# Sums of squares kept in PSUM, GpSimd adding pairs of chunks, and a softmax mixed with the first fold

## The chip, the core and the metric

The kernel runs on one core of one Trainium2 chip. The time is the device time of one execution in microseconds (us); the kernel before was run three times. A profiled execution of the same program gives the trace from which all rows below come. The engines are TensorE (PE, with its weight loads as PEld), VectorE (DVE), ScalarE (ACT), GpSimd (POOL) and SyncE (SP), which issues the loads.

## What is computed

A channel attention over 6016 tokens of 256 channels, and then two feed-forward layers:

```python
qn = q / (np.linalg.norm(q, axis=1, keepdims=True) + 1e-06)   # norm over the tokens
kn = k / (np.linalg.norm(k, axis=1, keepdims=True) + 1e-06)
s = kn.transpose(0, 2, 1) @ qn / tau                          # 256 x 256 scores
a = np.exp(s - s.max(-1, keepdims=True))
a /= a.sum(-1, keepdims=True) + 1e-09
x = (v @ a).reshape(B * S, D)
g = x @ w_gate                                                # first layer, 256 -> 1536 -> 256
x = silu(g) * (x @ w_val) @ w_out
h = x @ w_in                                                  # second layer, 256 -> 2048 -> 256
out = (h * np.clip(h + 3.0, 0.0, 6.0) / 6.0) @ w_out
```

The weights come as 64-bit floats and are turned into 32-bit ones on the chip.

## The kernel before

The order of each engine's instructions is written out by hand: the program issues them in the order of the code, and nothing reorders them.

**Prologue.** `q` and `k` come in 47 tiles of 128 tokens, grouped in 18 chunks (of 1, 2, 2, then thirteen of 3, then 2 and 1 tiles), numbered from 0. Eight chunks are under way at a time; SyncE issues them on one queue, with the first weight blocks between them. For each chunk ScalarE writes the squares of `tq` and `tk` into a tile `sq`, VectorE adds `sq` to the accumulator `acc` (128 x 1536 for a full chunk), and TensorE multiplies `tk` by `tq` into the scores `s` (two products a tile, each of which shows as two MATMUL records). VectorE folds `acc` from three tiles to one at the end. TensorE then adds over the partitions (`ss`), while the last tiles' score products wait behind it (three tiles; the constant `AFTER_SS`). From `ss` come the norms (ScalarE's root, VectorE's reciprocals `rno` and diagonal `dg`), TensorE spreads them over the partitions (`bc`, copied by ScalarE to `bc_sb`), VectorE scales the scores and takes the row maxima, ScalarE the exponentials, TensorE transposes them half by half (`tp`, copied to `et` in the tile `early`), and *folds* the attention matrix into the first weights (`ps_a`, `ps_d`), so that `v @ a` is never computed on its own.

**Weight blocks.** A block of 64-bit weights (`raw`, a job) passes through steps: `cut` (two VectorE instructions that take exponent `e` and mantissa `m` apart), `power` (two ScalarE instructions on `e`), `mantissa` and `sign` (VectorE on `m`), together the `fields`, and `scale` (VectorE, `m` times `e`). The function `pump` starts the fields of the next block; `PUMP_AT` says behind which chunk. Two blocks are needed for the first fold, the third and fourth soon after.

**The stretch after it.** The first layer starts with a plain product over 24 units, with later folds and weight blocks between them, and goes on in the seven-product scheme for two by two blocks for both layers. TensorE carries every product as three passes of 32-bit halves.

Of the kernel before, what the change touches and what calls it, by code (L numbers as in the profile page):

```python
# [18 lines left out]
def channel_attention_then_two_ffns(  # L19
# [24 lines left out]
    nc = tc.nc  # L44
# [405 lines left out]
    with tc.manual_schedule():  # L450

        with tc.tile_pool(name="sm", bufs=1) as sm, tc.tile_pool(name="qk", bufs=AHEAD) as qk_p, tc.tile_pool(
            name="sqp", bufs=3
        ) as sq_p:
            QC = 3
# [16 lines left out]

            LOAD_AT = {5: 1, 7: 2}
            PUMP_AT = {5: 1, 7: 2}

            AFTER_SS = 3
            WARM = 3
            ones = sm.tile([P, P], F32, name="ones")
            nc.vector.memset(ones, 1.0)

            def keep_warm(n):

                ps = ps_f.tile([P, P], F32, tag="b0", name="warm")
# [3 lines left out]
            loaded = []  # L487
# [4 lines left out]
            nc.sync.dma_start(out=tau_sb, in_=tau.to_broadcast([P, 1]))  # L492
            ident = sm.tile([P, P], F32, name="ident")
# [6 lines left out]

            s_ps = [ps_acc.tile([P, C], F32, tag=f"acc{i}", name=f"s{i}") for i in range(CT)]
# [36 lines left out]
            def square_sums():  # L538

                ss_ps = ps_acc.tile([P, 2 * CT], F32, tag="acc2", name="ss")  # L540
# [36 lines left out]

            nc.scalar.activation(warm, ones[:, 0:1], AF.Sqrt)
            squares(0)
            for i, (n0, n) in enumerate(chunks):  # L580
                if i + AHEAD < len(chunks):
                    loaded.append(load_qk(i + AHEAD))
                if i + AHEAD == len(chunks):
                    vraw = load_v(0)
                    load_jobs(RAW)
                squares(i + 1)
                sq = sqs.pop(i)
                nc.vector.tensor_tensor(out=acc[:, :n], in0=acc[:, :n], in1=sq[:, :n], op=ALU.add)
                if i == len(chunks) - 2:
                    nc.vector.tensor_tensor(out=acc[:, 1], in0=acc[:, 1], in1=acc[:, 2], op=ALU.add)  # L590
# [19 lines left out]
            bc_ps = ps_acc.tile([P, C], F32, tag="acc3", name="bc")  # L610
# [11 lines left out]
            for c in range(CT):  # L622
# [11 lines left out]
                )  # L634


            def transposed(c):
                tp = ps_f.tile([P, CT, P], F32, tag=f"b{c}", name="tp")
                for d in range(CT):
                    nc.tensor.transpose(tp[:, d, :], ex[:, c, d * P : (d + 1) * P], ident)  # L640
                nc.vector.tensor_scalar(
                    out=et[:, :, c * P : (c + 1) * P], in0=tp, scalar1=1.0, scalar2=None, op0=ALU.mult
                )

# [10 lines left out]

            transposed(0)
            transposed(1)
# [9 lines left out]
            jobs[2].mantissa()  # L667
            jobs[2].sign()
            passed[1] = 3
            load_jobs()  # L670
            nc.scalar.activation(warm, three, AF.Silu)
            jobs[2].power([1])
            passed[2:] = [3, 3]


        w1_p = ctx.enter_context(tc.tile_pool(name="w1", bufs=1))
        h_p = ctx.enter_context(tc.tile_pool(name="h", bufs=5))
        hl_p = ctx.enter_context(tc.tile_pool(name="hl", bufs=4))

# [7 lines left out]
        FA = [op_p.tile([P, 2 * CT, CW], F32, tag=f"op{i}", name="FA") for i in (7, 2)]  # L687
        FS = [op_p.tile([P, 2 * CT, CW], F32, tag=f"op{i}", name="FS") for i in (8, 1)]

        def first_fold():  # L690

            for c, ps in enumerate(fold_ps):
# [12 lines left out]
                v_lo(1, c)  # L705
            jobs[2].scale()
            for c, ps in enumerate(fold_ps):
# [311 lines left out]
        scaling = {i + 1: j for i, j in fields.items()}  # L1019
        third = fields.pop(0)  # L1020
        scaling.pop(1)
# [37 lines left out]
        for i, (f, b) in enumerate(units):  # L1059
# [31 lines left out]
            if i == 1:  # L1091
                jobs[third].power()
                jobs[third].mantissa()
                jobs[third].sign()
                passed[1] += 1
                load_jobs()
# [12 lines left out]
            if i == 0:  # L1109
                jobs[third].cut()  # L1110
            h_of = (f, b, h)
# [121 lines left out]
```

## Time and profile before

| | |
|---|---|
| three runs | 1096.37, 1097.02, 1097.03 us |
| profiled execution | 1096.71 us, span 1094.9 us |
| TensorE busy | 1085.6 us of the span |
| VectorE, ScalarE, GpSimd busy | 800.3, 759.8, 78.0 us |

The span runs from the first to the last instruction; the profiled execution's own time has 1.8 us more around it. Times in the trace count from the span's start. A MATMUL's recorded duration is longer than its share of TensorE, since they overlap; how many stand in a stretch tells more.

### The profile page before, as it was taken

Reading aid. Unit: us, or ns where it says so; the run is one execution under the profiler, and the core shown is the slowest. Engines: PE = TensorE matmul, PEld = TensorE weight load, DVE = VectorE, ACT = ScalarE, POOL = GpSimd, SP = SyncE. Lnnn points to the kernel's source line nnn. Section 1 sums busy time; section 2 is a strip of 40 time slices with the busy share of each in tenths; the row PEclk is TensorE's granted clock in tenths of the full one; section 3 lists DMA queues with packets and bytes.
Section 4 is the critical chain, followed back from the end, with each engine's and each line's share of the span. In section 5 each row is a group of like instructions: output and inputs, shape, how many; then the busy total and the mean of one; then the engine's idle time right before and its main releaser. Section 6 shows DMA issues by size and latency. Waiting matters only on the chain.

```text
span 1094.9 us, 13730 instructions
## 1 busy us (share of the span) xinstructions
PE 1085.6 (99%) x4878; PEld 915.2 (84%) x4878; DVE 800.3 (73%) x1259; ACT 759.8 (69%) x1319; POOL 78.0 (7%) x92
## 2 busy tenths in 40 slices
PE   8999999999999999999999999999999999999998
PEld 7888888888888888888888888888888888888997
DVE  6998995776776777677666677687687687686665
ACT  6776666667667776776765676776776776776765
POOL 0000000112221122122100000000000000000000
PEclk9999999999999999999999999999999999999999
DMA  9533303237346337426664724224225225224100
GB/s 353 214 96 101 111 1 114 76 120 259 106 145 225 109 128 245 146 95 224 211 231 184 305 97 159 91 97 169 82 97 172 79 96 173 73 85 151 39 1 34
DMA packets 63860, 150.31 MB, mean 137 GB/s; under 512 B 5168, under 2 KB 30896, under 8 KB 63024
## 3 DMA queue, kind: packets, MB, share of 16 engines
q1 hardware_dynamic: 63216, 148.67, 38.2%
q8 instruction: 38, 0.62, 0.2%
q10 hardware_dynamic: 576, 0.77, 0.2%
q14 instruction: 30, 0.25, 0.1%
HBM read 89.78 MB, written 59.64 MB: 136 GB/s over the span
## 4 chain that ended last, share of the span: by engine, by line
PE 95%; DMA 4%; DVE 1%; ACT 0%; issue 0%; SPq 0%; DVEq 0%
PE o L112 41%; PE ps_b L112 23%; PE ps_a L112 15%; PE ps_d L112 14%; DMA tk<-in_k 2%; DMA tq<-in_q 1%; PE ps_b L647 1%; DMA raw<-in_moe_w_gate 1%; PE ps_d L647 1%; PE ps_a L647 0%; DVE w L737 0%; DVE early L168 0%; ACT w L732 0%; DVE s_sb L623 0%; DVE nmx L631 0%
## 5 line engine op out<-in xcount | busy, mean ns | idle before, releaser
L875 DVE TENSOR_TENSOR hl<-h,hl 128x512 fp32r<-128x512 f32 (+2 forms) x312 | 210.4, 687 | 156.1 <-ACT hl L809 150.4
L112 PE MATMUL o<-hl,w2o 128*128 128x512 f32 (+1 forms) x1152 | 287.8, 385 | 0.0
L112 PEld LDWEIGHTS o<-hl,w2o 128*128 128x128 f32 x1152 | 215.8, 188 | 41.1 <-DVE hl L875 1.0
L809 ACT ACTIVATE hl<-h 128x512 fp32r<-128x512 f32 (+2 forms) x312 | 187.6, 617 | 58.0 <-DVE h L859 53.5
L112 PE MATMUL o<-hl,wo 128*128 128x496 f32 (+1 forms) x864 | 217.0, 386 | 0.0
L112 PEld LDWEIGHTS o<-hl,wo 128*128 128x128 f32 x864 | 162.2, 188 | 29.7
L112 PE MATMUL ps_b<-op,w 128*128 128x496 f32 (+1 forms) x540 | 139.3, 384 | 0.0
L112 PEld LDWEIGHTS ps_b<-op,w 128*128 128x128 f32 x540 | 101.3, 188 | 18.5 <-ACT ps_b L809 0.4
L112 PE MATMUL ps_b<-op,w2i 128*128 128x512 f32 (+1 forms) x432 | 112.0, 385 | 0.0
L813 DVE TENSOR_TENSOR h<-h,ps_d 128x512 f32<-128x512 f32 (+2 forms) x108 | 72.6, 672 | 51.5 <-PE ps_d L112 48.4
L809 ACT ACTIVATE h<-ps_b 128x512 f32<-128x512 f32 (+2 forms) x108 | 63.5, 588 | 65.6 <-PE ps_b L112 64.6
L809 ACT ACTIVATE ps_b<-ps_a 128x512 f32<-128x512 f32 (+2 forms) x108 | 61.8, 572 | 54.9 <-PE ps_a L112 54.9
L112 PE MATMUL ps_a<-op,w 128*128 128x496 f32 (+1 forms) x360 | 99.2, 384 | 0.0
L112 PE MATMUL ps_d<-op,w 128*128 128x496 f32 (+1 forms) x360 | 99.2, 384 | 0.0
L853 ACT ACTIVATE h<-h,three 128x512 f32<-128x512 f32 (+1 forms) x96 | 68.7, 716 | 40.3 <-DVE h L813 39.0
L112 PEld LDWEIGHTS ps_b<-op,w2i 128*128 128x128 f32 x432 | 81.1, 188 | 15.1
L813 DVE TENSOR_TENSOR h<-h,ps_b 128x512 f32<-128x512 f32 (+2 forms) x108 | 72.6, 672 | 9.9 <-PE ps_b L112 8.1
L112 PE MATMUL ps_a<-op,w2i 128*128 128x512 f32 (+1 forms) x288 | 79.7, 385 | 0.0
L112 PE MATMUL ps_d<-op,w2i 128*128 128x512 f32 (+1 forms) x288 | 79.7, 385 | 0.0
L112 PEld LDWEIGHTS ps_a<-op,w 128*128 128x128 f32 x360 | 67.6, 188 | 12.1
L112 PEld LDWEIGHTS ps_d<-op,w 128*128 128x128 f32 x360 | 67.6, 188 | 12.1
L859 DVE SCALAR_TENSOR_TENSOR h<-h 128x512 f32<-128x512 f32 (+1 forms) x96 | 65.1, 678 | 12.5 <-ACT h L853 12.5
(139 smaller groups left out, 1298.0 us busy)
## 6 DMA issues: line engine op xcount, KB each, us to landing
op<-opd SPq DMA_DIRECT2D x35, 512.0 KB, 4.3
opd<-sp SPq DMA_DIRECT2D x28, 496.0 KB, 2.7
op<-opd SPq DMA_DIRECT2D x28, 496.0 KB, 5.4
opd<-sp SPq DMA_DIRECT2D x21, 512.0 KB, 2.6
raw<-in_moe_w_out SPq DMA_DIRECT2D x14, 512.0 KB, 4.1
w2i<-wi_d SPq DMA_DIRECT2D x4, 1792.0 KB, 7.8
opd<-st SPq DMA_DIRECT2D x14, 512.0 KB, 2.6
x2r<-x_d SPq DMA_DIRECT2D x10, 512.0 KB, 4.7
```

The lines of the kernel that those rows point to most:

```text
L112: nc.tensor.matmul(out, lhsT=w, rhs=x, start=first, stop=last, skip_group_check=True)
L647: nc.tensor.matmul(out, lhsT=et[:, d, c * P : (c + 1) * P], rhs=wf[m, g][:, d, :], start=start and d == 0, stop=d == CT - 1, skip_group_ch ...
L809: nc.scalar.activation(out[:, : self.n], src[:, : self.n], AF.Copy)
L813: nc.vector.tensor_tensor(out=out[:, :n], in0=a[:, :n], in1=b[:, :n], op=ALU.add)
L853: nc.scalar.activation(r[:, : self.n], x[:, : self.n], AF.Relu, bias=three)
L859: nc.vector.scalar_tensor_tensor(out=r[:, :n], in0=r[:, :n], scalar=6.0, in1=x[:, :n], op0=ALU.min, op1=ALU.mult)
L875: nc.vector.tensor_tensor(out=hl[:, 1, :n], in0=h[:, :n], in1=hl[:, 0, :n].bitcast(F32), op=ALU.subtract)
```

## The change

- The accumulator of the squares is a PSUM tile of three banks, `acc_ps`, set to zero by VectorE; the add of chunk 15 writes its sum to the SBUF tile `acc`, and the last two chunks and the folds go on there.
- GpSimd adds the squares of chunk pairs (4,5), (7,8) and (10,11); VectorE adds each sum to `acc_ps` two chunks later.
- Four small matmuls of ones stand first on TensorE, and the three that stood ahead of the transposes are gone.
- The first two weight blocks are loaded behind chunks 8 and 10 instead of ahead of chunks 5 and 7, `tau` behind chunk 9; their fields stand behind chunks 8 and 11, and their `scale`, which stood behind the last add, behind chunks 12 and 13.
- Five tiles' products stand behind `ss` instead of three.
- The third block's `mantissa` and both steps of `power` stand ahead of the scores' scaling, its `sign` and `scale` inside the softmax. The first half is transposed and folded ahead of the second half's exponentials; ScalarE copies its transpose. The fourth block's steps stand earlier.

```diff
-    ps_acc = ctx.enter_context(tc.tile_pool(name="ps_acc", bufs=1, space=PSUM))
...
-            name="sqp", bufs=3
-        ) as sq_p:
+            name="sqp", bufs=6
+        ) as sq_p, tc.tile_pool(name="ps_s", bufs=1, space=PSUM) as ps_s:
...
-            LOAD_AT = {5: 1, 7: 2}
-            PUMP_AT = {5: 1, 7: 2}
-
-            AFTER_SS = 3
-            WARM = 3
+            LOAD_AT = {0: 1, 2: 2}
+            PUMP_AT = {8: 1, 11: 2}
+            SCALE_AT = {12: 0, 13: 1}
+            PAIRED = (5, 8, 11)
+            PAIR_LAG = 2
+
+            AFTER_SS = 5
+            WARM = 4
...
-            for i in range(AHEAD):
-                load_jobs(LOAD_AT.get(i, 0))
-                loaded.append(load_qk(i))
+            keep_warm(WARM)
+            loaded = [load_qk(i) for i in range(AHEAD)]
...
+            acc_ps = ps_s.tile([P, QC, 2, C], F32, tag="acc", name="acc_ps")
+            nc.vector.memset(acc_ps, 0.0)
             acc = sm.tile([P, QC, 2, C], F32, name="acc")
-            nc.gpsimd.memset(acc, 0.0)
...
                 squares(i + 1)
-                sq = sqs.pop(i)
-                nc.vector.tensor_tensor(out=acc[:, :n], in0=acc[:, :n], in1=sq[:, :n], op=ALU.add)
+                if i + 1 not in PAIRED:
+                    sq = sqs.pop(i)
+                    if i in PAIRED:
+                        first = sqs.pop(i - 1)
+                        nc.gpsimd.tensor_tensor(out=first, in0=first, in1=sq, op=ALU.add)
+                        paired[i + PAIR_LAG] = first
+                    else:
+                        a = acc if i > len(chunks) - 3 else acc_ps
+                        out = acc if i >= len(chunks) - 3 else acc_ps
+                        nc.vector.tensor_tensor(out=out[:, :n], in0=a[:, :n], in1=sq[:, :n], op=ALU.add)
+                if i in paired:
+                    nc.vector.tensor_tensor(out=acc_ps, in0=acc_ps, in1=paired.pop(i), op=ALU.add)
...
                 if i in PUMP_AT:
                     pump(PUMP_AT[i], steps=(1,), load=False)
+                    load_jobs(RAW if i > AHEAD else 0)
+                if i in SCALE_AT:
+                    jobs[SCALE_AT[i]].scale()
...
-            jobs[0].scale()
-            jobs[1].scale()
             jobs[2].cut()
+            jobs[2].mantissa()
             v_hi(0)
             v_hi(1)
             norms(ss_ps)
+            jobs[2].power()
...
-            jobs[2].power([0])
             for j, i in tiles[-AFTER_SS:]:
                 matmuls([j], i, [1])
-            keep_warm(WARM)
...
+                if c == 0:
+                    transposed(0)
+                    jobs[2].sign()
+                    passed[1] = 3
+                    load_jobs()
...
+            jobs[2].scale()
             fold_ps = [ps_f.tile([P, 2, CW], F32, tag="ad"[c], name="ps_" + "ad"[c]) for c in range(CT)]
             for c, ps in enumerate(fold_ps):
                 for m in range(2):
 
                     folding(ps[:, m, :], m, 0, c, m == 0)
+                    if not c and not m:
+                        transposed(1)
```

VectorE in the middle of the prologue, before the change: `acc` is the accumulator, `raw` a weight block, its four rows are the fields.

```order
L588 TENSOR_TENSOR acc<-acc,sq 128x1536 x3
L133 TENSOR_SCALAR e<-raw 128x512
L136 TENSOR_SCALAR m<-raw 128x512
L149 SCALAR_TENSOR_TENSOR m<-raw,m 128x512
L155 SCALAR_TENSOR_TENSOR m<-raw,m 128x512
L588 TENSOR_TENSOR acc<-acc,sq 128x1536 x2
```

After the change, from the add of the pair (4,5) (L603 adds a pair, L601 a chunk) to that of the pair (7,8) and the second block's fields:

```order
L603 TENSOR_TENSOR acc_ps<-acc_ps,sq 128x1536
L132 TENSOR_SCALAR e<-raw 128x512
L135 TENSOR_SCALAR m<-raw 128x512
L148 SCALAR_TENSOR_TENSOR m<-raw,m 128x512
L154 SCALAR_TENSOR_TENSOR m<-raw,m 128x512
L601 TENSOR_TENSOR acc_ps<-acc_ps,sq 128x1536
L603 TENSOR_TENSOR acc_ps<-acc_ps,sq 128x1536
L132 TENSOR_SCALAR e<-raw 128x512
L135 TENSOR_SCALAR m<-raw 128x512
L148 SCALAR_TENSOR_TENSOR m<-raw,m 128x512
L154 SCALAR_TENSOR_TENSOR m<-raw,m 128x512
```

The fields stand behind later chunks, and fewer adds stand between them. The end of the adds on VectorE, before the change, from the last eight full chunks to the two `scale` (`early`):

```order
L588 TENSOR_TENSOR acc<-acc,sq 128x1536 x8
L588 TENSOR_TENSOR acc<-acc,sq 128x1024
L590 TENSOR_TENSOR acc<-acc 128x512
L591 TENSOR_TENSOR acc<-acc 128x512
L588 TENSOR_TENSOR acc<-acc,sq 128x512
L597 TENSOR_SCALAR half<-half,tau_sb 128x2
L168 TENSOR_TENSOR early<-m,e 128x512 x2
```

After the change, from the add of chunk 12 to that of chunk 17:

```order
L601 TENSOR_TENSOR acc_ps<-acc_ps,sq 128x1536
L167 TENSOR_TENSOR early<-m,e 128x512
L601 TENSOR_TENSOR acc_ps<-acc_ps,sq 128x1536
L603 TENSOR_TENSOR acc_ps<-acc_ps,sq 128x1536
L167 TENSOR_TENSOR early<-m,e 128x512
L601 TENSOR_TENSOR acc_ps<-acc_ps,sq 128x1536
L601 TENSOR_TENSOR acc<-acc_ps,sq 128x1536
L605 TENSOR_TENSOR acc<-acc 128x512
L601 TENSOR_TENSOR acc<-acc,sq 128x1024
L607 TENSOR_TENSOR acc<-acc 128x512
L601 TENSOR_TENSOR acc<-acc,sq 128x512
```

The two `scale` moved ahead of the last adds, and the pair (10,11) stands between chunks 13 and 14. ScalarE behind `ss`, before the change, from the root to the exponentials of both halves:

```order
L553 ACTIVATE nrm<-ss,tiny 128x4
L554 ACT_TABLE_LOAD
L554 ACTIVATE warm<-tiny 128x1
L613 ACTIVATE bc_sb<-bc 128x256
L143 ACTIVATE e<-e,exp_top 128x512
L632 ACTIVATE s_sb,den<-s_sb,nmx 128x256 x2
```

After the change (L142 and L144 are the third block's `power`):

```order
L554 ACTIVATE nrm<-ss,tiny 128x4
L555 ACT_TABLE_LOAD
L555 ACTIVATE warm<-tiny 128x1
L142 ACTIVATE e<-e,exp_top 128x512
L144 ACTIVATE e<-e,exp_span 128x512
L632 ACTIVATE bc_sb<-bc 128x256
L659 ACTIVATE s_sb,den<-s_sb,nmx 128x256
L642 ACTIVATE early<-tp 128x2x128
L659 ACTIVATE s_sb,den<-s_sb,nmx 128x256
```

Both steps of `power` stand ahead of `bc_sb`, and the copy of the first transpose between the two exponentials.

## Rows read from the trace of the kernel before

**Rows 1.** The page's first part: busy time, share of the span, instructions.

```profile
PE 1085.6 (99%) x4878; PEld 915.2 (84%) x4878; DVE 800.3 (73%) x1259; ACT 759.8 (69%) x1319; POOL 78.0 (7%) x92
```

**Rows 2.** Chain that ended last, first 60 us: start, length, what.

```profile
54.34 2.77 PE ps_b L112 x12
```

**Rows 3.** TensorE's timeline, 42 to 55 us: start, length, what, count.

```profile
44.07 0.95 PE L542 MATMUL ss<-ones,acc 128*128 128x1 f32 x8
46.78 0.71 PE L612 MATMUL bc<-dg,ones 128*128 128x128 f32 x4 [0.36 <-DVE dg L561]
...
50.73 1.89 PE L647 MATMUL ps_a<-early 128*128 128x256 f32 x8
```

**Rows 4.** Score MATMULs alone, by stretch: busy (count), granted clock, DMA.

```profile
3.50:7.90 4.40, 4.32 (x10) 1.00 1.01 362
8.20:22.80 14.60, 14.60 (x69) 1.00 0.99 385
```

**Rows 5.** Timeline, ScalarE's squares of chunks 4, 5, 6, 8 and 12.

```profile
10.47 0.85 ACT L521 ACTIVATE sq<-tq 128x768 f32<-128x768 f32 x1 [0.19 <-DMA tq<-in_q]
...
13.66 0.84 ACT L521 ACTIVATE sq<-tq 128x768 f32<-128x768 f32 x1 [1.48 <-DMA tq<-in_q]
...
15.53 0.84 ACT L521 ACTIVATE sq<-tq 128x768 f32<-128x768 f32 x1 [0.16 <-DMA tq<-in_q]
...
22.18 0.84 ACT L521 ACTIVATE sq<-tq 128x768 f32<-128x768 f32 x1 [1.38 <-DMA tq<-in_q]
...
30.74 0.84 ACT L522 ACTIVATE sq<-tk 128x768 f32<-128x768 f32 x1
```

**Rows 6.** Timeline, VectorE: first block's fields, later adds, last add, two `scale`.

```profile
17.08 0.42 DVE L133 TENSOR_SCALAR e<-raw 128x512 uint32<-128x512 uint32 x1
...
19.21 3.61 DVE L588 TENSOR_TENSOR acc<-acc,sq 128x1536 f32<-128x1536 f32 x2
...
26.87 14.26 DVE L588 TENSOR_TENSOR acc<-acc,sq 128x1536 f32<-128x1536 f32 x8 [0.25 <-ACT sq L522]
...
42.69 0.69 DVE L588 TENSOR_TENSOR acc<-acc,sq 128x512 f32<-128x512 f32 x1
...
43.43 1.28 DVE L168 TENSOR_TENSOR early<-m,e 128x512 f32<-128x512 f32 x2
```

**Rows 7.** GpSimd's groups by shape: count, busy us, mean ns, idle before.

```profile
L209 POOL TENSOR_TENSOR st<-m,st 128x512 fp32r<-128x512 f32 x8 | 10.4, 1295 | 92.8 <-ACT st L215 92.8
...
L209 POOL TENSOR_TENSOR st<-m,st 128x256 fp32r<-128x256 f32 x8 | 6.0, 753 | 80.9 <-ACT st L220 80.9
```

**Rows 8.** Line 866, 270 to 310 us (min/median/max ns); timeline, 299 to 305 us.

```profile
L866 DVE TENSOR_TENSOR h<-h x6: 676/892/1139, 271.3 to 307.8; 128x496 f32<-128x496 f32 x6
...
299.52 0.67 DVE L813 TENSOR_TENSOR h<-h,ps_b 128x496 f32<-128x496 f32 x1
299.61 1.29 POOL L168 TENSOR_TENSOR m<-m,e 128x512 f32<-128x512 f32 x1 [6.04 <-DVE m L155]
...
300.29 1.14 DVE L866 TENSOR_TENSOR h<-h 128x496 f32<-128x496 f32 x1
...
301.83 0.47 POOL L198 TENSOR_TENSOR e<-e,m 128x128 f32<-128x128 f32 x1
...
302.25 0.90 POOL L199 TENSOR_TENSOR e<-m 128x128 f32<-128x128 f32 x1
302.75 0.93 DVE L357 TENSOR_TENSOR sp<-vr,sp 128x496 fp32r<-128x496 f32 x1
```

**Rows 9.** Timeline, ScalarE from the root to `power` of the third block.

```profile
45.05 0.27 ACT L553 ACTIVATE nrm<-ss,tiny 128x4 f32<-128x4 f32 x1 [2.80 <-PE ss L542]
45.34 1.28 ACT L554 ACT_TABLE_LOAD   x1
...
47.53 0.38 ACT L613 ACTIVATE bc_sb<-bc 128x256 f32<-128x256 f32 x1 [0.69 <-PE bc L612]
47.81 0.71 ACT L143 ACTIVATE e<-e,exp_top 128x512 f32<-128x512 uint32 x1
```

More of the change, by code (lines that the diff above doesn't have):

```diff
@@ L481, in keep_warm @@
             def keep_warm(n):
-                ps = ps_f.tile([P, P], F32, tag="b0", name="warm")
+                ps = ps_f.tile([P, P], F32, tag="a", name="warm")
                 for _ in range(n):
                     nc.tensor.matmul(ps, lhsT=ones, rhs=ones, start=True, stop=True)
-            loaded = []
-            for i in range(AHEAD):
-                load_jobs(LOAD_AT.get(i, 0))
-                loaded.append(load_qk(i))
+            keep_warm(WARM)
+            loaded = [load_qk(i) for i in range(AHEAD)]
             tau_sb = sm.tile([P, 1], F32, name="tau_sb")
-            nc.sync.dma_start(out=tau_sb, in_=tau.to_broadcast([P, 1]))
             ident = sm.tile([P, P], F32, name="ident")
@@ L499, in channel_attention_then_two_ffns @@
             nc.gpsimd.memset(exp_span, 4.0 * (EXP_TOP - EXP_LOW))
-            s_ps = [ps_acc.tile([P, C], F32, tag=f"acc{i}", name=f"s{i}") for i in range(CT)]
+            assert QC == 3 and CT * C == TB
+            s_ps = [ps_f.tile([P, C], F32, tag=f"b{i}", name=f"s{i}") for i in range(CT)]
+            acc_ps = ps_s.tile([P, QC, 2, C], F32, tag="acc", name="acc_ps")
+            nc.vector.memset(acc_ps, 0.0)
             acc = sm.tile([P, QC, 2, C], F32, name="acc")
-            nc.gpsimd.memset(acc, 0.0)
             half = sm.tile([P, 2 * CT], F32, name="half")
@@ L538, in square_sums @@
             def square_sums():
-                ss_ps = ps_acc.tile([P, 2 * CT], F32, tag="acc2", name="ss")
+                ss_ps = ps_f.tile([P, 2 * CT], F32, tag="a", name="ss")
                 for m in range(2 * CT):
@@ L578, in channel_attention_then_two_ffns @@
             nc.scalar.activation(warm, ones[:, 0:1], AF.Sqrt)
+            paired = {}
             squares(0)
@@ L582, in channel_attention_then_two_ffns @@
                     loaded.append(load_qk(i + AHEAD))
+                if i == 1:
+                    nc.sync.dma_start(out=tau_sb, in_=tau.to_broadcast([P, 1]))
+                load_jobs(LOAD_AT.get(i, 0))
                 if i + AHEAD == len(chunks):
@@ L586, in channel_attention_then_two_ffns @@
                 squares(i + 1)
-                sq = sqs.pop(i)
-                nc.vector.tensor_tensor(out=acc[:, :n], in0=acc[:, :n], in1=sq[:, :n], op=ALU.add)
+                if i + 1 not in PAIRED:
[10 more added lines that the diff above has]
+                    nc.vector.tensor_tensor(out=acc_ps, in0=acc_ps, in1=paired.pop(i), op=ALU.add)
+                if i == len(chunks) - 3:
+                    nc.vector.tensor_tensor(out=acc[:, 0], in0=acc[:, 0], in1=acc[:, 2], op=ALU.add)
                 if i == len(chunks) - 2:
-                    nc.vector.tensor_tensor(out=acc[:, 1], in0=acc[:, 1], in1=acc[:, 2], op=ALU.add)
                     nc.vector.tensor_tensor(out=acc[:, 0], in0=acc[:, 0], in1=acc[:, 1], op=ALU.add)
@@ L613, in channel_attention_then_two_ffns, with transposed @@
             nc.scalar.activation(bc_sb, bc_ps, AF.Copy)
-            jobs[2].power([0])
             for j, i in tiles[-AFTER_SS:]:
                 matmuls([j], i, [1])
-            keep_warm(WARM)
+            def transposed(c):
+                tp = (ps_s, ps_f)[c].tile([P, CT, P], F32, tag="td"[c], name="tp")
+                for d in range(CT):
+                    nc.tensor.transpose(tp[:, d, :], ex[:, c, d * P : (d + 1) * P], ident)
+                out = et[:, :, c * P : (c + 1) * P]
+                if c == 0:
+                    nc.scalar.activation(out, tp, AF.Copy)
+                else:
+                    nc.vector.tensor_scalar(out=out, in0=tp, scalar1=1.0, scalar2=None, op0=ALU.mult)
             nmx = sm.tile([P, CT], F32, name="nmx")
@@ L634, in channel_attention_then_two_ffns @@
                 )
[L637 to L643, printed above, removed]
+                if c == 0:
+                    transposed(0)
+                    jobs[2].sign()
+                    passed[1] = 3
+                    load_jobs()
             def folding(out, m, g, c, start):
@@ L666, in channel_attention_then_two_ffns @@
             v_lo(0, 1)
[L667 to L670, printed above, removed]
             nc.scalar.activation(warm, three, AF.Silu)
-            jobs[2].power([1])
             passed[2:] = [3, 3]
@@ L677, in channel_attention_then_two_ffns @@
         h_p = ctx.enter_context(tc.tile_pool(name="h", bufs=5))
+        ps_acc = ctx.enter_context(tc.tile_pool(name="ps_acc", bufs=1, space=PSUM))
         hl_p = ctx.enter_context(tc.tile_pool(name="hl", bufs=4))
@@ L688, in channel_attention_then_two_ffns @@
         FS = [op_p.tile([P, 2 * CT, CW], F32, tag=f"op{i}", name="FS") for i in (8, 1)]
+        third = at[1, 1]
         def first_fold():
@@ L705, in first_fold @@
                 v_lo(1, c)
-            jobs[2].scale()
+            jobs[third].cut()
+            jobs[third].mantissa()
             for c, ps in enumerate(fold_ps):
@@ L1019, in channel_attention_then_two_ffns @@
         scaling = {i + 1: j for i, j in fields.items()}
-        third = fields.pop(0)
+        assert fields.pop(0) == third
         scaling.pop(1)
@@ L1091, in channel_attention_then_two_ffns @@
             if i == 1:
-                jobs[third].power()
-                jobs[third].mantissa()
                 jobs[third].sign()
@@ L1109, in channel_attention_then_two_ffns @@
             if i == 0:
-                jobs[third].cut()
+                jobs[third].power()
             h_of = (f, b, h)
```

4 lines of the change are left out of this document (1 added, 3 removed).

## The prediction

> **What bounds the kernel now.** Read the page's first part, then the chain of waits, then each engine's timeline up to the point where TensorE stops waiting. TensorE is busy 99% of the span [rows 1], and the chain in order of time runs on TensorE alone, in pieces that touch, from 54.34 us [rows 2]. So the sum is the shift of that moment: everything that the change touches stands ahead of it or beside a TensorE that is never idle.
>
> Before 54.34 three engines matter. TensorE: the sums `ss` start at 44.07, the broadcast `bc` at 46.78, the first fold at 50.73 [rows 3]. The fold is 6.66 us after `ss` and the steady stretch 10.27 after it. TensorE ran late into `ss`: its first ten score MATMULs fill 4.4 us, 0.43 each, and 69 later ones 14.6, 0.21 each [rows 4]. That is the lower of its two levels against the higher, after a start without work; the granted clock column reads 1.00 in both. VectorE: its last add ends at 43.38 (42.69 + 0.69), and from 26.87 on adds stand back to back, 14.26 us for seven full chunks and one of two tiles, so 1.86 for a full chunk with the gap before it and 1.33 for the other [rows 6]. Loads: a chunk's squares begin when `tq` lands; chunks 5 and 6 are 1.87 us apart, a weight block adds 1.32 (10.47 to 13.66 is 3.19) [rows 5]. From chunk 6 (15.53) to chunk 8 (22.18) are two chunks, one block and 1.59 us more, where `tau` travels [rows 5].
>
> **The change on VectorE ahead of `ss`.** This sets the end, because `ss` needs the finished `acc`.
>
> The bytes ahead of chunk 12 are the same as before, only in another order, so its squares end at 31.6 as now (30.74 + 0.84) [rows 5]. Behind them stand five full adds (chunks 12 and 13, the pair (10,11), 14, 15), 9.3 us; the two `scale`, 1.28; two folds of `acc` at 0.73, 1.46; chunk 16, 1.33; chunk 17, 0.79: together 14.1 us [rows 6]. In the kernel before, four full adds and no `scale` follow chunk 12. Even if VectorE stood ready and idle for chunk 12, `acc` would be done at 45.7, against 43.38. The pairs save three adds, 5.6 us, but they save them where VectorE now waits for loads, and one of them comes back after chunk 12.
>
> I expect VectorE not to be ready. GpSimd's add of 512 elements takes 1.295 us and of 256 0.753 [rows 7], so 1536 take an estimated 1.295 + 4 x 0.542 = 3.46 us. Beside GpSimd, VectorE's instructions with two SBUF inputs wait: `h<-h`, 0.68 at the least, took 1.14 us started at 300.29 under a GpSimd add that ends at 300.90; GpSimd's add at 302.25 waited in turn, 0.90 instead of the 0.47 of its like at 301.83, and the VectorE instruction that came at 302.75 waited behind that one, 0.93 [rows 8]. So the two alternate, whole instruction by whole instruction. The VectorE instruction with a PSUM input at 299.52 kept its 0.67 [rows 8]. The adds into `acc_ps` have one SBUF input and go on beside GpSimd; the weight steps (`cut`, `mantissa`, `sign`, `scale`) work from SBUF to SBUF and don't. No row shows `cut` beside GpSimd. Its bounds: no wait, or the whole rest of the add; I take the wait, as its nearest rows are the SBUF ones.
>
> The Trainium skill (SBUF — State Buffer, "Who interferes with whom") states the same rule against this change: the second port pair of VectorE is GpSimd's, held for a whole instruction, by VectorE instructions with two SBUF inputs and by single-input ones in the two-port modes. The rows agree for two inputs; by the rule `cut` waits too, and the sum is the one below.
>
> With [rows 5] the new order gives chunk 8's `tq` at 10.47 + 4 x 1.87 = 17.95 and its squares done at 19.7 (half a chunk, 0.94, more for `tk`, and 0.84). GpSimd then adds (7,8) from 19.75 to 23.2. The first weight block lands at 20.2, inside that add, so its fields, 2.13 us (17.08 to 19.21) [rows 6], run 23.2 to 25.3 instead of 20.2 to 22.3. Chunk 9 and the pair (7,8), 3.7 us: 29.0. The second block's `cut`, 0.67: 29.7. Chunk 11's squares end at 17.95 + 3 x 1.87 + 2 x 1.32 + 1.59 + 0.94 + 0.84 = 29.6, and GpSimd's add (10,11) wants the port then. Whichever of it and `mantissa` goes first, at least `sign` stands behind 3.46 us of GpSimd and the fields end at 34.1 to 34.5; I take 34.2. Then the 14.1 us: `acc` is done at 48.3, and `ss` starts at 48.4, 4.3 us later than now.
>
> **TensorE ahead of `ss`.** Five tiles instead of three stand behind `ss`, 8 MATMULs of 0.21 less ahead of it, 1.7 us; warm matmuls first save between nothing and 2.1 us (ten MATMULs at 0.43 instead of 0.21) [rows 4]. TensorE is then through by 40.3 to 42.4: hidden, since `acc` is later. But TensorE now stands idle for some 6 us before `ss`, more than the 3.5 us at the start of the span behind which it ran at 0.43 [rows 4]. Price of the lower level, if it lasts 4.4 us again: `ss` 0.8 us more, then six of the ten score MATMULs at 0.43, and `bc` can start 5.3 us behind `ss` instead of 3.1. ScalarE hides part of that (next paragraph): 1.9 us. Its bounds are 0 and 1.9; I take 1.9.
>
> **From `ss` to the steady stretch.** On VectorE `cut` and `mantissa` of the third block (0.7 + 0.7) lie beside `ss` and the square root, where two `scale` (1.28) and `cut` lie now [rows 6]. On ScalarE both steps of `power` now stand ahead of `bc_sb`: root at 0.99 behind `ss`, 0.27; table 1.28; 0.2; two steps of 0.71; `bc_sb` starts 4.15 us behind `ss` instead of 3.46 (47.53 - 44.07) [rows 3, 9], 0.7 later. From `bc_sb` to the first fold are 3.2 us now; by halves it is one row of `s_sb`, maximum, exponential, transpose and copy instead of two maxima in a row: 2.9, 0.3 earlier. The fold itself takes 0.1 more, for the transposes of the second half inside it. Sum: + 0.5.
>
> **At nothing**: the memset of `acc_ps` (VectorE has no other work until the first squares), `tau` and the weight loads in another place (same bytes, same queue), the third block's steps earlier or later beside steady TensorE [rows 2]. Without that cover the third block's `cut` and `mantissa` ahead of the first low parts would cost 1.4 us once.
>
> **Sum**: 4.3 + 0.5 + 1.9 = 6.7 us. The profiled execution took 1096.71 us with a span of 1094.9; its median is 0.3 above, inside the 0.66 by which the runs differ. 1096.7 + 6.7 = 1103.4.
>
> **Rivals.**
> *The lower level doesn't come.* For it: four warm matmuls and a long busy stretch ahead. Against: 6 us without work. 1101.5. The Trainium skill (TensorE: Matmul & The Clock Gate, "What's actually happening") says that an idle TensorE returns to the lower level by default, which would favour my sum.
> *GpSimd doesn't hold the fields*, or the order at 29.6 falls the other way (`cut` runs beside GpSimd, and `sign` is through before the second add). VectorE then waits for chunk 12, `acc` ends at 45.7 to 46.6, and the total is 1099.0 to 1099.9, or with the lower level up to 1101.8. For it: half a microsecond decides at 29.6.
> *Faster: adds into PSUM are quicker than adds in SBUF.* Place: VectorE's tail after chunk 12. At two elements a cycle, as `cut` runs (0.42 against 0.69 for 512 elements) [rows 6], five adds cost 4 us less, `acc` ends near 41.5, TensorE's own end at 41 to 42 takes over, and the total is about 1095. It decides from `acc` at 43.4: there TensorE's 0.6 us of lateness in the kernel before pays for the 0.5 of the later stretch, so the tail must shrink below 11.8 us. Against: an add with a PSUM input takes 0.67 for 496 elements [rows 8], like one without.
> *Worse*: a wait I don't see ahead of `acc`, over 1104.8.
>
> **How the numbers follow.** My forecast 0.40; without the lower level 0.15; fields not held 0.27; faster or about equal, up to 1098, 0.12; worse 0.06. The predicted time is 1103.4. The range 1098.0 to 1104.8 leaves out the last two, 0.18. What a measurement tells from no change is about 0.2%, 2.2 us: under 1094.8 lies a third to half of the fast case, 0.05; up to 1099.2 the rest of it and part of the third case, 0.17; above, 0.78.
>
> **What would show it.** After the change `cut` of the first block should start or last until GpSimd's first long add under it ends, about 23; `sign` of the second until about 33.5; the last add before `ss` should end near 48, TensorE stand idle from 42, and score MATMULs behind `ss` take 0.43. The first fold should come 7 us or more behind `ss`. I am wrong if the add of chunk 12 waits for squares, if adds into `acc_ps` take far less than 1.76, or if steady TensorE starts before 56.

## The result and the profile after

The changed kernel took 1101.97 us (median of five runs, 1100.94 to 1104.57) against 1096.99 before: ratio 1.0053, with a 95% interval of 1.0038 to 1.0067. It is slower, by 5.0 us. Its profiled execution took 1101.89 us with a span of 1100.1, 5.2 more than before on both counts. The five runs lie 3.6 us apart, those of before 0.7. The mean granted clock of TensorE recorded with them is 0.998 in the fastest, 0.997 in the next three and 0.995 in the slowest; the section on the prediction comes back to that spread.

The page's first part and the chain of waits (start, length, what), against [rows 1, 2]:

```profile
PE 1089.7 (99%) x4880; PEld 918.6 (84%) x4880; DVE 799.8 (73%) x1256; ACT 761.2 (69%) x1320; POOL 87.4 (8%) x94
```

```profile
59.81 2.76 PE ps_b L111 x12
```

The steady stretch starts at 59.81 instead of 54.34. From there to the end of the span are 1040.3 us, and were 1040.6. The whole loss lies ahead of that moment.

VectorE's timeline (start, length, line, what, and in brackets the idle time before it and its releaser), from the first block's fields to chunk 13, and then the last add:

```profile
19.81 3.33 DVE L132 TENSOR_SCALAR e<-raw 128x512 uint32<-128x512 uint32 x1 [0.62 <-DMA raw<-in_moe_w_gate]
...
26.71 1.77 DVE L603 TENSOR_TENSOR acc_ps<-acc_ps,sq 128x1536 f32<-128x1536 f32 x1
28.39 0.42 DVE L132 TENSOR_SCALAR e<-raw 128x512 uint32<-128x512 uint32 x1
...
29.91 0.69 DVE L154 SCALAR_TENSOR_TENSOR m<-raw,m 128x512 uint32<-128x512 uint32 x1
31.74 1.77 DVE L601 TENSOR_TENSOR acc_ps<-acc_ps,sq 128x1536 f32<-128x1536 f32 x1 [1.14 <-ACT sq L523]
33.41 1.05 DVE L167 TENSOR_TENSOR early<-m,e 128x512 f32<-128x512 f32 x1
...
45.22 0.69 DVE L601 TENSOR_TENSOR acc<-acc,sq 128x512 f32<-128x512 f32 x1
```

The same view of GpSimd, its three pair adds:

```profile
13.74 3.45 POOL L596 TENSOR_TENSOR sq<-sq 128x1536 f32<-128x1536 f32 x1 [12.25 <-ACT sq L523]
19.42 3.44 POOL L596 TENSOR_TENSOR sq<-sq 128x1536 f32<-128x1536 f32 x1 [2.23 <-ACT sq L523]
29.99 3.92 POOL L596 TENSOR_TENSOR sq<-sq 128x1536 f32<-128x1536 f32 x1 [7.13 <-ACT sq L523]
```

Read the two together. `cut` of the first block needs 0.42 us [rows 6] and is recorded with 3.33: it ends 0.28 behind GpSimd's second add (19.42 + 3.44 = 22.86). A held instruction shows as a long one, not as idle time. The second block's `sign` (L154) is the case on which the prediction turned: it starts at 29.91, GpSimd's third add at 29.99, and it is GpSimd that waits (3.92 instead of 3.45). So the fields end at 30.60, VectorE stands idle 1.14 us for chunk 12's squares, and only the first `scale` is held, 1.05 instead of 0.68. The last add ends at 45.91, 2.53 later than before. (Between the two blocks' fields stand two adds, as many as before the change.)

TensorE's timeline around `ss`, against [rows 3]:

```profile
41.65 0.59 PE L570 MATMUL s<-tq,tk 128*128 128x256 f32 x2
46.06 1.84 PE L543 MATMUL ss<-ones,acc 128*128 128x1 f32 x8 [3.82 <-DVE half L616]
47.76 4.60 PE L570 MATMUL s<-tq,tk 128*128 128x256 f32 x10
52.16 0.64 PE L631 MATMUL bc<-dg,ones 128*128 128x128 f32 x4
...
55.87 1.13 PE L670 MATMUL ps_a<-early 128*128 128x256 f32 x4 [0.47 <-ACT early L642]
```

and TensorE by stretch (length, busy time with its count, granted clock, DMA share, GB/s):

```profile
42.30:46.00 3.70, 0.00 (x0) 0.92 0.02 7
46.00:47.80 1.80, 1.74 (x9) 0.50 0.00 0
47.80:52.20 4.40, 4.40 (x12) 0.50 0.00 2
52.20:54.70 2.50, 2.50 (x15) 1.00 0.00 0
```

TensorE is through with its products at 42.24 and stands idle 3.8 us. Toward the end of that the granted clock falls from 1.00 to 0.50, the lower level (1.2 GHz): its mean of 0.92 over 3.7 us is an estimated 0.6 us at 0.50. It stays there until 52.2, 6.2 us from the start of `ss`, through `ss` (1.84 instead of 0.95) and all ten products. `bc` starts 6.1 us behind `ss` instead of 2.7.

### The profile page after: what moved, and what is told of

Its sections match the earlier page's. It is cut to its first block, busy times and chain, and to the rows that moved or that the text cites. A ratio compares the mean times of both kernels' runs of the same rounds, so it can differ in the third digit from the quotient of the medians.

```text
span 1100.1 us, 13728 instructions
## 1 busy us (share of the span) xinstructions
PE 1089.7 (99%) x4880; PEld 918.6 (84%) x4880; DVE 799.8 (73%) x1256; ACT 761.2 (69%) x1320; POOL 87.4 (8%) x94
## 4 chain that ended last, share of the span: by engine, by line
PE 94%; DMA 3%; DVE 2%; ACT 1%; issue 0%; ACTq 0%; DVEq 0%; SPq 0%
PE o L111 40%; PE ps_b L111 23%; PE ps_a L111 14%; PE ps_d L111 14%; DMA tk<-in_k 2%; PE ps_b L670 1%; PE ps_d L670 1%; PE s L570 1%; DMA tq<-in_q 1%; PE ps_a L670 0%; DVE acc L601 0%; DVE acc_ps L601 0%; PE ss L543 0%; DVE acc_ps L603 0%; ACT sq L523 0%
```

## The experiments

In each, the moment to compare is the first fold's start behind `ss`: 6.66 us before [rows 3], 9.81 in the changed kernel (55.87 - 46.06). Where the softmax goes by halves the steady stretch follows 3.94 behind it (59.81 - 55.87).

**TensorE kept busy ahead of `ss`.**

```diff
+            keep_warm(16)
             ss_ps = square_sums()
```

> The changed kernel with sixteen more matmuls of ones (about 3.5 us at the higher level) on TensorE between the last score product ahead of the sums and the sums themselves, so that it is not idle while the accumulator is finished. Nothing of the result depends on them. Theory A, the idle time ahead of ss costs the clock: ss starts at 46.06 as in the changed kernel, its eight MATMULs follow each other at 0.11 instead of 0.21, the scores behind it at 0.22 instead of 0.43, bc comes 2.7 us behind ss instead of 6.1; then ScalarE's two steps of power are last and bc_sb starts about 4.15 behind ss; first fold 53.2, steady stretch 57.2 instead of 59.8, time 1099.3. Theory B, the ten score MATMULs ahead of bc or the steps of power are what is late, whatever TensorE did before: bc stays over 5 us behind ss, steady stretch from 59 on, time 1101 to 1102.

Measured: 1101.49 us (1100.07 to 1104.27), ratio 1.0042 (1.0030 to 1.0053). Until 41.8 us this is the changed kernel, instruction by instruction; still its profiled execution (1103.86) went another way at 30 us. VectorE, GpSimd, and TensorE by stretch:

```profile
30.33 3.84 DVE L154 SCALAR_TENSOR_TENSOR m<-raw,m 128x512 uint32<-128x512 uint32 x1
34.10 1.75 DVE L601 TENSOR_TENSOR acc_ps<-acc_ps,sq 128x1536 f32<-128x1536 f32 x1
```

```profile
19.85 3.44 POOL L596 TENSOR_TENSOR sq<-sq 128x1536 f32<-128x1536 f32 x1 [2.23 <-ACT sq L523]
29.64 3.98 POOL L596 TENSOR_TENSOR sq<-sq 128x1536 f32<-128x1536 f32 x1 [6.35 <-ACT sq L523]
```

```profile
45.50:47.80 2.30, 0.07 (x1) 1.00 0.00 0
47.80:48.50 0.70, 0.66 (x5) 0.77 0.00 0
48.50:54.90 6.40, 6.40 (x20) 0.50 0.01 4
```

Here GpSimd asked at 29.64, during `mantissa`, got its turn behind it, and held `sign` for 3.84 us. Chunk 12's add starts at 34.10 instead of 31.74 and the last add ends at 47.70. That is the order on which the prediction's sum rests. What differs is when chunks landed and were squared, which shows in when GpSimd starts: its second add, beside the first `cut`, 0.43 us later than in the changed kernel's trace (19.85 against 19.42), its third 0.35 earlier (29.64 against 29.99).

As a test of the clock the trace fails: the accumulator came 1.8 us later, the sixteen matmuls were over at 45.6, and the level fell within `ss`, behind 2.3 us without work. The six runs say a little more: three kept a mean granted clock of 1.000 and are the three fastest (1100.07 to 1101.17 us), the other three had 0.997 or 0.998 (1101.80 to 1104.27). Which order each of them took at 30 us is not known.

**`scale` back behind the last add.**

```diff
-            SCALE_AT = {12: 0, 13: 1}
+            SCALE_AT = {}
...
+            jobs[0].scale()
+            jobs[1].scale()
             jobs[2].cut()
```

> The changed kernel with the scale of the first two blocks back behind the last add. Both theories: accumulator done at about 44.2 instead of 45.9, ss at 44.3, TensorE idle 2.1 us ahead of it instead of 3.8. Theory A, the lower level comes after this idle time too: bc 6.1 behind ss, steady stretch at 58.0, time 1100.1. Theory B, it takes a longer idle time: bc waits for VectorE, which does two scale, cut and mantissa first (rno not before 46.9), so bc at 48.4 and bc_sb at 49.0, steady stretch 56.0, time 1098.1.

Measured: 1102.75 us (1102.59 to 1104.01), ratio 1.0052 (1.0040 to 1.0064). Again `sign` stood behind GpSimd (30.22, 3.90 us), so that the last add ended at 46.85 and TensorE was idle 5.3 us; the lower level came as before. The run doesn't tell A from B. It is the second trace with the order of the prediction.

**No pairs.**

```diff
-            PAIRED = (5, 8, 11)
+            PAIRED = ()
```

> The changed kernel without pairs: GpSimd adds nothing, VectorE adds every chunk into PSUM. Theory A, the three adds that GpSimd takes over are given back (one add stands behind chunk 12, fields and a scale are held): the fields of the first block run from 21.1 without a hold, those of the second end at 33.8, behind that four full adds and two scale: the accumulator is done at about 46.1 against 45.9, time 1102.1, the same as the changed kernel. Theory B, the pairs save what they take off VectorE (5.6 us): accumulator past 50, time 1106 or more. Theory C, they cost: accumulator at or under 45.3, time 1101.3 or less.

Measured: 1101.07 us (1099.91 to 1101.77), ratio 1.0033 (1.0021 to 1.0045). VectorE's adds of chunks 11, 12 and 17 and the second `sign`, and TensorE:

```profile
29.77 1.77 DVE L601 TENSOR_TENSOR acc_ps<-acc_ps,sq 128x1536 f32<-128x1536 f32 x1 [1.37 <-ACT sq L523]
...
32.98 0.69 DVE L154 SCALAR_TENSOR_TENSOR m<-raw,m 128x512 uint32<-128x512 uint32 x1
33.59 1.76 DVE L601 TENSOR_TENSOR acc_ps<-acc_ps,sq 128x1536 f32<-128x1536 f32 x1
...
44.63 0.69 DVE L601 TENSOR_TENSOR acc<-acc,sq 128x512 f32<-128x512 f32 x1
```

```profile
45.47 1.69 PE L543 MATMUL ss<-ones,acc 128*128 128x1 f32 x8 [3.15 <-DVE half L616]
...
55.55 1.13 PE L670 MATMUL ps_a<-early 128*128 128x256 f32 x4 [0.47 <-ACT early L642]
```

With all adds on VectorE the accumulator is done at 45.32, 0.6 earlier than in the changed kernel's profile and 2.4 earlier than where `sign` is held. By the accumulator it is theory C: the pairs cost. They take adds off VectorE where it waits for loads anyway (1.37 us ahead of chunk 11's add), so that three adds less bring chunk 12's add forward by 1.85 us only (31.74 against 33.59), and the one add that they leave behind chunk 12 costs 1.86 again; the held `scale` comes on top. In the times alone it is not clear of noise: the two intervals, 1.0021 to 1.0045 here and 1.0038 to 1.0067 for the changed kernel, overlap. The runs also lie closer together (1.9 us).

**The accumulator in SBUF.**

```diff
-            acc_ps = ps_s.tile([P, QC, 2, C], F32, tag="acc", name="acc_ps")
+            acc_ps = sm.tile([P, QC, 2, C], F32, name="acc_ps")
```

> The changed kernel with the accumulator in SBUF in place of PSUM, all else as it is. Theory A, adds with one PSUM input run beside GpSimd and adds with two SBUF inputs wait for it: the add of chunk 6 (15.56) lasts until GpSimd's first add ends at 17.2, GpSimd's second add waits for VectorE's, the second block's fields or the add of chunk 12 stand behind the third; accumulator done at about 49.6, 3.7 later, time about 1105.6. Theory B, the place of the accumulator makes no difference beside GpSimd: the add of chunk 6 takes 1.77, accumulator at 45.9, time 1102.

Measured: 1104.77 us (1104.29 to 1106.41), ratio 1.0072 (1.0059 to 1.0085). VectorE and GpSimd:

```profile
15.41 3.27 DVE L601 TENSOR_TENSOR acc_ps<-acc_ps,sq 128x1536 f32<-128x1536 f32 x1 [3.89 <-ACT sq L523]
...
33.30 3.33 DVE L601 TENSOR_TENSOR acc_ps<-acc_ps,sq 128x1536 f32<-128x1536 f32 x1 [1.72 <-ACT sq L523]
```

```profile
19.26 4.58 POOL L596 TENSOR_TENSOR sq<-sq 128x1536 f32<-128x1536 f32 x1 [2.20 <-ACT sq L523]
31.56 3.46 POOL L596 TENSOR_TENSOR sq<-sq 128x1536 f32<-128x1536 f32 x1 [7.71 <-ACT sq L523]
```

Theory A. With two SBUF inputs the adds of chunks 6 and 12 take 3.27 and 3.33 us instead of 1.77, and GpSimd's second add waits in turn (4.58). The last add ends at 48.47, 2.56 later than in the changed kernel (3.7 was expected). So a PSUM input is what lets VectorE add beside GpSimd, and it buys nothing for a single add (1.77 against 1.76).

**No pairs, and TensorE busy until `ss`.** Without the pairs the accumulator's end no longer depends on who asks first, so the clock can be tested alone.

```diff
-            PAIRED = (5, 8, 11)
+            PAIRED = ()
...
+            keep_warm(14)
             ss_ps = square_sums()
```

> The changed kernel without pairs (accumulator at 45.3, whichever way GpSimd would go) and with fourteen matmuls of ones ahead of ss, 3.1 us, so that TensorE works from its last score product until ss. To compare with the run without pairs alone (ss at 45.47, bc 6.0 behind it, steady stretch at 59.5). Theory A, the idle time ahead of ss costs the clock: ss MATMULs 0.11 apart, scores 0.22, bc 2.7 behind ss, then ScalarE's two steps of power are last and bc_sb starts 4.15 behind ss; first fold at 52.6, steady stretch at 56.5, 3.0 earlier, time 1098. Theory B, the order behind ss is what is late: bc still over 5 behind ss, no difference.

Measured: 1098.75 us (1098.29 to 1100.92), ratio 1.0019 (1.0010 to 1.0028); against the kernel before, run beside each, that is 1.8 us more (1096.95), where without the fourteen matmuls it was 3.5 more (1101.07 against 1097.54). The profiled executions lie 3.4 apart (1098.41 against 1101.77). TensorE, then ScalarE:

```profile
45.10 1.02 PE L543 MATMUL ss<-ones,acc 128*128 128x1 f32 x8
45.99 2.40 PE L570 MATMUL s<-tq,tk 128*128 128x256 f32 x10
48.23 0.61 PE L632 MATMUL bc<-dg,ones 128*128 128x128 f32 x4
...
52.21 1.13 PE L671 MATMUL ps_a<-early 128*128 128x256 f32 x4 [0.47 <-ACT early L643]
```

```profile
49.21 0.36 ACT L633 ACTIVATE bc_sb<-bc 128x256 f32<-128x256 f32 x1
```

Theory A. `ss` and the products run at the higher level, and the first fold comes 7.11 us behind `ss` instead of 10.08 without the matmuls (55.55 - 45.47). The lower level costs 2.97 us in this pair of traces; by the medians it is less, 1.7 (3.5 against 1.8). The mean granted clock recorded with each run agrees: 0.999 or 1.000 in ten of these eleven runs, 0.997 or 0.998 in all five without the matmuls.

**One tile behind `ss`.** Real work in place of the matmuls of ones: four more tiles' products ahead of `ss`, no pairs.

```diff
-            PAIRED = (5, 8, 11)
+            PAIRED = ()
...
-            AFTER_SS = 5
+            AFTER_SS = 1
```

> The changed kernel without pairs and with one tile's products behind ss instead of five: TensorE works on until about 44.0 and stands idle 1.5 us instead of 3.2. Theory A, the clock falls only behind the longer idle time: bc 2.7 behind ss, bc_sb 4.15, first fold at 52.4, steady stretch at 56.4, time 1098. Theory B, it falls after any such idle time: two scores instead of ten stand ahead of bc, so bc about 3.9 behind ss, bc_sb 4.6, steady stretch about 57.2, time 1098.8. Theory C, the clock has nothing to do with it: as theory A, so that this run alone does not tell A from C.

Measured: 1100.63 us (1100.19 to 1101.93), ratio 1.0036 (1.0022 to 1.0050). TensorE by stretch, and its first fold:

```profile
44.00:45.60 1.60, 1.60 (x9) 1.00 0.00 0
45.60:48.50 2.90, 1.73 (x12) 1.00 0.00 0
...
49.20:52.00 2.80, 0.87 (x4) 0.50 0.00 0
```

```profile
53.12 2.07 PE L670 MATMUL ps_a<-early 128*128 128x256 f32 x4 [0.47 <-ACT early L642]
```

All three theories missed, and so did what they share, an idle time ahead of `ss`: the products lasted until it came. `ss` ran at the higher level, but with little left to do TensorE then waited 1.2 us for `bc` and 1.9 for the transposes, and the level fell between the two waits: four MATMULs of the fold took 2.07 instead of 1.13. The idle time was moved behind `ss`, and the price went with it.

**Nine matmuls of ones first.**

```diff
-            WARM = 4
+            WARM = 9
```

> The changed kernel with nine matmuls of ones first instead of four, so that they last from 1.05 to about 4.9, past the landing of the first chunk. Theory A, the higher level comes with work that is not broken off, matmuls of ones count: the scores begin 1.2 later but at 0.22 instead of 0.43, the ten are done at about 7.1 instead of 8.0. Theory B, they don't count or not enough: ten scores at 0.43 as before, done at about 9.2. In neither case does the end move, since the accumulator is later: 1101 to 1104.

Measured: one run, 1102.43 us. TensorE by stretch:

```profile
5.00:7.20 2.20, 2.20 (x13) 1.00 1.01 381
```

The changed kernel's four end at 3.13 and leave 0.54 us without work ahead of the first products, which then run at 0.43 as before [rows 4]. Nine reach past that point, and the products from 5.03 on run at 0.22: ten are done at 7.2 instead of 8.0. That looks like theory A, but two other traces take it back. The run above without pairs and with TensorE busy until `ss` has four first, as the changed kernel, and its first twelve products are done at 7.03 (timeline):

```profile
3.60 3.43 PE L570 MATMUL s<-tq,tk 128*128 128x256 f32 x12 [0.48 <-DMA tk<-in_k]
```

The last version below has nine first, and only seven MATMULs stand in its 2 us from 5.0 on, where thirteen stand in the 2.2 us above:

```profile
5.00:7.00 2.00, 2.00 (x7) 1.00 0.97 348
```

So the moment at which the level rises differs between executions with the same start, and one run doesn't tell A from B. As expected the end did not move (1101 to 1104), since `ss` waits for VectorE.

**`power` behind `bc_sb`.** On top of no pairs and a busy TensorE:

```diff
-            jobs[2].power()
             v_lo(0, 0)
...
             nc.scalar.activation(bc_sb, bc_ps, AF.Copy)
+            jobs[2].power()
```

> The run without pairs and with TensorE busy until ss (1098.4 in its profile; ss at 45.10, bc at 48.23, bc_sb 4.11 behind ss), with both steps of power of the third block behind bc_sb instead of ahead of it. Theory A, the steps are what ends last there: bc_sb starts when bc is done, 3.85 behind ss, a quarter of a microsecond earlier (the ten score MATMULs ahead of bc hide the rest of the 0.7), and the first fold and the steady stretch move by as much unless the exponentials now wait for power: 1098.2. Theory B, no change of bc_sb: 1098.4.

Measured: 1099.38 us (1098.43 to 1101.80), ratio 1.0024 (1.0014 to 1.0033), no less than with `power` ahead: 2.3 us above the kernel before, run beside it (1097.09), instead of 1.8. (Its two slowest runs, 1101.53 and 1101.80, have a mean granted clock of 0.998, the others 0.999 or 1.000.) `ss` started at 45.31; ScalarE behind it:

```profile
49.12 0.38 ACT L632 ACTIVATE bc_sb<-bc 128x256 f32<-128x256 f32 x1 [0.93 <-PE bc L631]
...
50.14 0.72 ACT L144 ACTIVATE e<-e,exp_span 128x512 uint32<-128x512 f32 x1
50.77 0.49 ACT L660 ACTIVATE s_sb<-s_sb,nmx 128x256 f32<-128x256 f32 x1
```

Theory A for `bc_sb`: 3.81 behind `ss` instead of 4.11. But the exponentials now stand behind the second step, and the first fold comes 7.07 behind `ss` instead of 7.11. Where `power` stands is worth nothing here.

**Only the rest of the change.** No pairs; loads, fields, `scale` and `power` back where the kernel before has them. The accumulator in PSUM, five tiles behind `ss`, the first matmuls and the halves stay.

```diff
-            LOAD_AT = {0: 1, 2: 2}
-            PUMP_AT = {8: 1, 11: 2}
-            SCALE_AT = {12: 0, 13: 1}
-            PAIRED = (5, 8, 11)
+            LOAD_AT = {5: 1, 7: 2}
+            PUMP_AT = {5: 1, 7: 2}
+            SCALE_AT = {}
+            PAIRED = ()
...
```

> What of the change neither delays the accumulator nor puts ScalarE ahead of bc_sb: no pairs, loads and fields where the kernel before has them, scale behind the last add, both steps of power where they were; kept are the accumulator in PSUM, five tiles behind ss, the warm matmuls first and the softmax by halves. Accumulator at 43.4 as in the kernel before, TensorE through at 42.2 instead of 44.0, so ss at 43.5 instead of 44.07, no lower level (1.3 us idle); bc 2.7 behind it, first fold at 50.0 instead of 50.73, steady stretch at 53.8 instead of 54.34: 1096.5, 0.5 under the kernel before. If the third block's steps are late instead, a wait shows behind 54 and the time is 1097 to 1098.

Measured: 1098.65 us (1097.37 to 1100.45), ratio 1.0015 (1.0006 to 1.0023). TensorE and VectorE in the profiled execution (1097.37):

```profile
43.63 1.02 PE L546 MATMUL ss<-ones,acc 128*128 128x1 f32 x8 [1.71 <-DVE acc L603]
44.51 2.40 PE L573 MATMUL s<-tq,tk 128*128 128x256 f32 x10
46.83 0.71 PE L633 MATMUL bc<-dg,ones 128*128 128x128 f32 x4
```

```profile
45.07 0.42 DVE L135 TENSOR_SCALAR m<-raw 128x512 uint32<-128x512 uint32 x1
45.40 0.17 DVE L559 RECIPROCAL rno<-nrm 128x4 f32<-128x4 f32 x1
```

The forecast of 1096.5 missed. `ss` is 0.44 earlier than before, and that gains nothing: `bc` comes at 46.83, as before at 46.78. VectorE has two `scale` and `cut` to do until 45.49, so that `rno` starts at 45.40 (before: at 45.35). And TensorE now has ten products instead of six ahead of `bc`, which also end there (44.51 + 2.40 = 46.91). Two chains run side by side up to `bc`, and neither of them ends earlier.

**The same with TensorE busy until `ss`.**

```diff
+            keep_warm(6)
             ss_ps = square_sums()
```

> The run that keeps only the rest of the change (no pairs, loads, fields, scale and power where the kernel before has them; it gave 1097.4 in four runs and 1098.2 to 1100.5 in seven, with ss at 43.63 behind 1.3 us without work), with six matmuls of ones ahead of ss that fill these 1.3 us. Theory A, the slower runs are those in which the clock falls behind the idle time: all runs near 1097.4, median 1 us or more lower. Theory B, they have another cause: the same spread, median 1098.6.

Measured: 1097.28 us (1096.86 to 1098.22), ratio 1.0002 (0.9993 to 1.0011). The median lies 0.2 us above that of the kernel before, run beside it (1097.09), instead of 1.7 (1098.65 against 1096.95), and the spread is 1.4 us instead of 3.1, as theory A has it. The profiled execution of the run without the six matmuls was its fastest, so that no trace shows the level fall in one of the longer ones. The mean granted clock recorded with each run does: the four runs up to 1097.59 us have 0.999 or 1.000, the seven from 1098.19 on 0.997 or 0.998, and all eleven with the six matmuls 0.999 or 1.000.

**A version of what helped.** All adds on VectorE into PSUM, `scale` on GpSimd behind chunks 9 and 10, nine matmuls first, three tiles behind `ss`, softmax, `power` and fold as before. The line of its edit that no other run has:

```diff
...
-                    jobs[SCALE_AT[i]].scale()
+                    jobs[SCALE_AT[i]].scale(nc.gpsimd)
...
```

> A version made of what helped: accumulator in PSUM with all adds on VectorE, loads and fields where the kernel before has them, the two scale on GpSimd behind chunks 9 and 10 (adds with a PSUM input do not wait for it) in place of VectorE behind the last add, nine matmuls of ones first, three tiles behind ss, softmax, power and fold in the order of the kernel before. Accumulator at 43.4, TensorE through at 43.1 instead of 44.0, ss at 43.6; VectorE has cut and mantissa beside it instead of two scale and cut, rno at 44.9 instead of 45.35, bc at 46.3, bc_sb at 47.1 instead of 47.53, steady stretch 53.9 instead of 54.34: 1096.5, 0.4 under the kernel before. If GpSimd's scale delays VectorE's adds all the same, accumulator at 44.5 or later and 1097.5.

Measured: 1096.90 us (1096.44 to 1097.28), ratio 0.9998 (0.9989 to 1.0007): no difference that can be measured. GpSimd's second `scale` and the adds beside it:

```profile
25.83 1.28 POOL L167 TENSOR_TENSOR early<-m,e 128x512 f32<-128x512 f32 x1 [4.37 <-DVE m L154]
```

```profile
25.61 3.62 DVE L603 TENSOR_TENSOR acc_ps<-acc_ps,sq 128x1536 f32<-128x1536 f32 x2
```

Neither holds the other, as hoped. But in this execution the last add ended at 44.02 and TensorE's own products at 44.12, not at 43.4 and 43.1, so `ss` started at 44.17 (before: at 44.07) and nothing was gained.

## Why the prediction came out as it did

The forecast was slower, 1103.4 us, in 1098.0 to 1104.8; the measurement is 1101.97. The sign holds, and so do the held `cut`, the tail behind chunk 12 and the lower level. The largest term, the wait of the second `sign`, did not come in the profiled execution, and the sum came near in part by luck: `ss` started 2.3 us earlier than forecast, and what follows it cost 0.8 more (3.2 instead of 2.4). In the profiled executions:

| term | predicted | measured |
|---|---|---|
| start of `ss` | + 4.3 | + 1.99 (46.06 - 44.07) |
| `ss` to the steady stretch, clock apart | + 0.5 | + 0.78 (7.11 + 3.94 - 10.27) |
| lower level | + 1.9 | + 2.70 (9.81 - 7.11) |
| behind the steady stretch's start | 0 | - 0.27 |
| sum | 6.7 | 5.2 |

**Fixed behind 54.34.** Right: 1040.3 us against 1040.6.

**GpSimd's add, 3.46 us, and `cut` held by it.** Right: 3.45 and 3.44, and `cut` until 23.14 where 23.2 plus its own time was counted. No row of before showed a one-input instruction held; this trace does. The Trainium skill (SBUF — State Buffer, "Who interferes with whom") counts such instructions in the two-port modes among those that wait, and says that whoever issues first has the ports for the whole instruction; the traces agree with both, in 3.33 us for `cut` and in the two orders at 30 us. That `cut` ran in such a mode the traces show by its pace alone (0.42 us where `sign` takes 0.69 for as many elements).

**The step that failed**: "Whichever of it and `mantissa` goes first, at least `sign` stands behind 3.46 us of GpSimd and the fields end at 34.1 to 34.5; I take 34.2." The first fields ended at 24.93 instead of 25.3, since `cut`'s own time lies inside its wait, and the second `cut` came at 28.39 instead of 29.0. `sign` then stood at 29.91, 0.08 ahead of GpSimd. The sum left out that order, in which both `mantissa` and `sign` go first, and chunk 12's add then waited 1.14 us for squares: by the prediction's own sign ("I am wrong if the add of chunk 12 waits for squares") its path was wrong there. The rival had named the place ("half a microsecond decides at 29.6"); what the sum took as settled is a race. Both outcomes occur with the same instructions on VectorE and GpSimd: `sign` first in the changed kernel's trace (last add 45.91) and in the run with nine matmuls first (29.98 against 30.48), GpSimd first in the first run of the experiments (47.70).

The 45.91 lies in the rival's 45.7 to 46.6, for which it has 1099.2, or 1101.1 with its 1.9 for the lower level. That the profiled execution came out at 1101.89, near the rival's bound of 1101.8, is luck: the lower level cost 0.8 more than counted. The spread of the changed kernel's five runs has two candidates: the order at 30 us, worth 1.8 us in the accumulator, and the length of the stretch at the lower level. A mean granted clock of 0.995 over 1102.8 us is an estimated 11 us at 0.50, one of 0.998 over 1099.2 an estimated 4.4. Which of the two made which run is not shown; the order is known for the profiled one alone.

**The tail behind chunk 12**, 14.1 us: right, 31.74 to 45.91 is 14.17 with 0.37 of held `scale` in it. Its start at the squares' end, 31.7 (31.6 before), too.

**TensorE ahead of `ss`.** Through at 42.24, inside 40.3 to 42.4, at the end at which the first matmuls save nothing. That holds for this execution: behind the same four the level rose sooner in others (see the run with nine matmuls).

**The lower level**: right in kind, mis-sized. It came in 3.8 us of idle time instead of 6. I let it end 4.4 us behind `ss`, as at the start of the kernel [rows 4], six products in; it ended 6.2 us behind `ss`, and all ten were done. By the Trainium skill (TensorE: Matmul & The Clock Gate, "What's actually happening") an idle TensorE returns to the lower level. The two runs without pairs agree: the granted clock fell where TensorE had stood idle for 3.15 us, not where it was kept busy, and 2.97 us lie between them in their traces.

**From `ss` to the steady stretch.** Where the clock held, `bc_sb` came 0.65 later behind `ss` (4.11 instead of 3.46), as counted, but `power` is only part of the cause: ten products instead of six now stand ahead of `bc`, which comes 3.13 behind `ss` (48.23 - 45.10) instead of 2.71. With `power` moved away `bc_sb` gained 0.30, and the first fold 0.04, since the exponentials then wait for it. The halves gain 0.2 from `bc_sb` to the first fold (52.21 - 49.21 against 50.73 - 47.53), not 0.3, and the fold lasts 0.33 longer (3.94 against 3.61), not 0.1. As built, the halves cost 0.1.

**Faster adds into PSUM**: refuted, 1.77 against 1.76.

## What to carry to other kernels

Before work is given to a second engine, see where the first one has no time to spare and where it waits anyway: three adds taken off VectorE ahead of chunk 12 brought that chunk's add forward by the length of one, and one added behind it cost its full length. When two engines hold each other off and their requests are forecast within a microsecond of each other, count both orders with a chance each: the same program went either way here. And a wait ahead of TensorE costs twice where its clock falls: follow the granted clock past the wait, and give the engine some work that holds it there, as fourteen spare matmuls did in ten runs of eleven.

## What the runs showed of the hardware

- VectorE's one-input `cut` on 32-bit integers, SBUF to SBUF, waited for the rest of GpSimd's add: 3.33 us for an instruction of 0.42. GpSimd waits in turn, 3.92 and 4.58 us for an add of 3.45.
- The level fell within `ss`, behind 2.3 us without work, in one run, and between waits of 1.2 and 1.9 us in another, while a few MATMULs ran.
- Matmuls of ones, which nothing reads, held the higher level in ten runs of eleven (fourteen ahead of `ss`).
- Behind the same start the level rises at different moments: with four matmuls of ones first, ten products were done at 8.0 us in one trace and twelve at 7.03 in another.
